# Attention stages at planned places of the expert chunks, batch 1's one unit later, query transposes ahead of the value bounce

## The chip, the cores and the metric

The kernel runs on one core of a Trainium2 chip. The metric is the device time of one execution in microseconds (us), lower is better; the median of three runs is given. The five engines are named as in the profile: PE (TensorE; PEld is its weight load), DVE (VectorE), ACT (ScalarE), POOL (GpSimd), SP (SyncE, which here only issues DMAs). A queue of an engine is worked off strictly in the order in which the program was written, except that a weight load may run ahead.

## The reference, cut to what matters

Sinkhorn-sorted block attention over 4 batches, 8 heads, 768 tokens, head size 64, in 8 blocks of 96 tokens, then 4 experts over 3072 tokens of width 512 with hidden width 1024.

```python
# P: [B,H,8,8], five rounds of softmax over rows and normalisation over columns
k_sorted = einsum('bhij,bhjcd->bhicd', P, k_blocks)   # v_sorted likewise
attn = softmax(q_b @ k_sorted_b.T / 8)                # inside a block of 96
x    = (attn @ v_sorted_b) -> [B*S, H*D]
p    = domain_probs / domain_probs.sum(-1)
out  = sum_e p[:, e] * (relu(x @ w1[e]) @ w2[e])
```

## The kernel before, in words

Batch 0's attention is done first (two halves), in a form of its own. From then on the experts' matmuls fill PE, and the attention of the next batch is put between them in pieces. Everything is scheduled by hand: an engine's queue has the order in which the Python code emits instructions.

**Batch 0's experts** are units `(b, e, hf)` run by `expert`: four groups `ps_h` (8 matmuls, 128x384 each, L548, evicted by ACT as relu) and three groups `ps_o` (8 matmuls of 512 columns, L562, evicted by DVE at L569/L573). A unit has 7 slots, one behind each group. Batch 1's attention is put into the slots of six units, (0,0,1) to (0,3,1).

**Batches 1 to 3** run as three chunks each of 256 tokens, `chunk(b, c)`: eight groups `ps_h` (16 matmuls, L636, two for each expert, evicted by DVE at L642 into `Hb` with relu and the token weights `pb`), then seven products of a Strassen-like scheme (`ps_p`, 16 matmuls each, L663) in the order p1, p4, p2, p5, p6, p7, p3. `h_sums(e, 1..4)` are DVE additions (L617 to L623) of blocks of `Hb` into `Sb`; the products p5, p6, p7 and p3 read sums 1, 2, 3 and 4. `weight_sums(e)` are the additions on the weights' side, on POOL (L596 to L599), one expert after the other. A chunk has 15 slots: one behind each of the 8 groups and of the 7 products. PSUM has two buffers `psM` for `ps_h`, `ps_o` and the products, and two `psA` for the attention.

**The attention stages** of one pair of heads `pr` (four pairs): `st_q` transposes q by a DMA from SP's queue (`qT<-natq`, L324). `st_v` mixes the blocks of v on PE (L298), evicts into `vo` (one buffer; DVE for batch 1, ACT otherwise), and after every second pair writes `vo` to `vs_dram` and reads it back as `vs`, both from SP's queue (L311, L316): the value bounce. `st_k` mixes k (L334), `st_s` makes scores and exponentials (L351, L358 on ACT), `st_a` multiplies by `vs` (L383) and normalizes on DVE (L367, L368), `st_x` transposes the result into `xT` by a DMA from SP. `load_natural` and `load_queries` fetch the next batch's v, k and q by DMAs from POOL's queue, as `load_w1` and `load_w2` do with the experts' weights (L114, L117).

`run` spreads a list of stages evenly over the slots of its units; `attention_order(b)` is that list. `spread_weights` normalizes the token weights of batches 1 to 3 (DVE L512 to L515), transposes them on PE (L530), writes them to `p_dram` (L533) and loads the first `pb` (L606). The same four operations of `normalized` are run on batch 0's smaller table `p_sb` during the start.

Of the kernel before, what the change touches and what calls it, by code (L numbers as in the profile page):

```python
# [17 lines left out]
def kernel(  # L18
# [13 lines left out]
    B, H, S, D = q.shape  # L32
# [4 lines left out]
    E = moe_w1.shape[0]  # L37
# [5 lines left out]
    R = BLK // CP  # L43
    NKC = Dm // P
    NFC = FF // P
    NPB = H // 2
# [39 lines left out]
    def load_natural(b, nm, qd, p0=0, pn=P):  # L86
        src = {"q": q, "k": k, "v": v}[nm]
        if b == 0 and nm == "q":
            natural[(b, nm, qd)] = q0[:, ds(4 * qd, 4)]
        elif (b, nm, qd) not in natural:  # L90
            natural[(b, nm, qd)] = nat.tile([P, 4, R, D], F16, name=f"nat_{nm}_{b}_{qd}", tag=f"nat_{nm}")
        t = natural[(b, nm, qd)]
        nc.gpsimd.dma_start(  # L93
            t[ds(p0, pn)].rearrange("p h r d -> p h (r d)"),
            src[b, ds(4 * qd, 4)].rearrange("h (p r) d -> p h (r d)", r=R)[ds(p0, pn)],
        )

    def load_queries(b):

        t = nat.tile([P, NPB, R, 2, D], F16, name=f"natq_{b}", tag="natq", bufs=1)  # L100
        natural[(b, "q")] = t
        for h in range(H):
            nc.gpsimd.dma_start(t[:, h // 2, :, h % 2, :], q[b, h].rearrange("(t p) d -> p t d", p=P))  # L103
# [369 lines left out]
    def h_x(qd, hf, copy):  # L473
# [8 lines left out]
            ps.rearrange("p n (r c) -> p r n c", c=CP),  # L482
        )

    def attention_order(b):
        o = [(st_v, 0), (st_v, 1), (st_q, 0), (st_k, 0), (st_v, 2), (st_v, 3)]
        for pr in range(NPB):
            o.append((st_s, pr))
            if pr + 1 < NPB:
                o += [(st_q, pr + 1), (st_k, pr + 1)]  # L490
            o.append((st_a, pr))
            o.append((st_x, pr))

        for pr in range(NPB - 1):
            o.remove((st_x, pr))
            o.insert(o.index((st_s, pr + 1)) + 1, (st_x, pr))

        def stage(f, pr):
            f(b, pr)
            nm = {st_k: "k", st_v: "v"}.get(f)  # L500
            if nm and pr % 2 and b + 1 < B:
                load_natural(b + 1, nm, pr // 2)
            if f == st_s and pr == NPB - 1 and b + 1 < B:
                load_queries(b + 1)

        return [lambda f=f, pr=pr: stage(f, pr) for f, pr in o]


    def normalized(p, n, name):
# [79 lines left out]
    def weight_sums(e):  # L589
        t = Tt[e]  # L590
        w = w2sb[e]
        b11, b12 = w[:, 0:KH, 0:DH], w[:, 0:KH, DH:Dm]
        b21, b22 = w[:, KH:NFC, 0:DH], w[:, KH:NFC, DH:Dm]
        t2, t3, n4 = t[:, 0], t[:, 1], t[:, 2]
        tt = nc.gpsimd.tensor_tensor
        tt(t3, b22, b12, ALU.subtract)  # L596
        tt(b12, b12, b11, ALU.subtract)
        tt(t2, b22, b12, ALU.subtract)
        tt(n4, b21, t2, ALU.subtract)  # L599
        Ts.append({  # L600
            "b11": b11, "b21": b21, "b22": b22, "t1": b12, "t2": t2, "t3": t3, "n4": n4,
        })
# [9 lines left out]
    def h_sums(e, which):  # L612
        blk = lambda kh, tok: Hb[:, e, ds(kh * KH, KH), ds(tok * P, P)]
        sm = [Sb[:, n, e].rearrange("p (f x) -> p f x", f=KH) for n in range(4)]
        tt = nc.vector.tensor_tensor
        if which == 1:
            tt(sm[0], blk(0, 1), blk(1, 1), ALU.add)  # L617
        elif which == 2:
            tt(sm[1], sm[0], blk(0, 0), ALU.subtract)
        elif which == 3:  # L620
            tt(sm[2], blk(0, 0), blk(0, 1), ALU.subtract)
        else:
            tt(sm[3], blk(1, 0), sm[1], ALU.subtract)  # L623
# [3 lines left out]
    def chunk(b, c, slot):  # L627

        xT = xTs[b].rearrange("p k i x -> p k (i x)")
        pb = pbs.pop((b, c))  # L630
        for e in range(E):
            for g in range(2):
                ps = psm([P, 4, 2 * P], F32, f"ps_h_{b}_{c}_{e}_{g}")
                for f in range(4):
                    for kc in range(NKC):
                        nc.tensor.matmul(  # L636
                            ps[:, f, :],
                            w1sb[e][:, kc, ds((4 * g + f) * P, P)],
                            xT[:, kc, ds(2 * c * P, 2 * P)],
                            start=(kc == 0), stop=(kc == NKC - 1),  # L640
                        )
                nc.vector.scalar_tensor_tensor(  # L642
                    out=Hb[:, e, ds(4 * g, 4), :], in0=ps[:], scalar=0.0,
                    op0=ALU.max, in1=pb[:, ds(e, 1), :].broadcast_to([P, 4, 2 * P]), op1=ALU.mult,
                )
                if e:
                    h_sums(e - 1, 1 + 2 * g)
                    h_sums(e - 1, 2 + 2 * g)
                slot()
        for w in range(1, 5):  # L650
            h_sums(E - 1, w)
        if (b, c) != (B - 1, R // 2 - 1):
            nxt = (b, c + 1) if c + 1 < R // 2 else (b + 1, 0)
            pbs[nxt] = load_p(*nxt)

        blk = lambda kh, tok: (lambda e, f: Hb[:, e, kh * KH + f, ds(tok * P, P)])
        sm = lambda n: (lambda e, f: Sb[:, n, e, ds(f * P, P)])

        def product(n, lhs, rhs):
            ps = psm([P, DH], F32, f"ps_{n}_{b}_{c}")  # L660
            for e in range(E):
                for f in range(KH):
                    nc.tensor.matmul(  # L663
                        ps[:], lhs(e, f), Ts[e][rhs][:, f, :],
                        start=(e == 0 and f == 0), stop=(e == E - 1 and f == KH - 1),
                    )
            slot()
            return ps[:]

        oa = moeo.tile([P, Dm], F32, name=f"oa_{b}_{c}", tag="oacc")  # L670
        ob = moeo.tile([P, Dm], F32, name=f"ob_{b}_{c}", tag="oacc")
        p1, p5, u2, u3 = [moe.tile([P, DH], F32, name=f"{n}_{b}_{c}", tag=n, bufs=1) for n in ("p1", "p5", "u2", "u3")]
        tt = nc.vector.tensor_tensor
        o = out[ds(b * S, S), :].rearrange("(t p) d -> p t d", p=P)
        oa1, oa2, ob1, ob2 = oa[:, 0:DH], oa[:, DH:Dm], ob[:, 0:DH], ob[:, DH:Dm]
        nc.scalar.copy(p1[:], product("p1", blk(0, 0), "b11"))  # L676
        nc.scalar.copy(ob1, product("p4", blk(1, 1), "n4"))
        tt(oa1, product("p2", blk(1, 0), "b21"), p1[:], ALU.add)
        nc.scalar.copy(p5[:], product("p5", sm(0), "t1"))
        tt(u2[:], product("p6", sm(1), "t2"), p1[:], ALU.add)  # L680
        nc.gpsimd.tensor_tensor(oa2, u2[:], p5[:], ALU.add)  # L681
        tt(u3[:], product("p7", sm(2), "t3"), u2[:], ALU.add)
        nc.gpsimd.tensor_tensor(ob2, u3[:], p5[:], ALU.add)
        tt(ob1, ob1, u3[:], ALU.add)
        nc.sync.dma_start(o[:, 2 * c + 1, :], ob[:])
        tt(oa2, product("p3", sm(3), "b22"), oa2, ALU.add)
        nc.sync.dma_start(o[:, 2 * c, :], oa[:])

    def run(units, slots, fill, spare=4):

        fill, total, done = list(fill), len(fill), [0, 0]

        def slot():
            done[0] += 1
            while fill and done[1] * (slots - spare) < done[0] * total:
                fill.pop(0)()
                done[1] += 1

        for u in units:
            u(slot)  # L700
        for f in fill:
            f()

    def halves(units):
        return [lambda slot, u=u: expert(*u, slot) for u in units]
# [44 lines left out]
    def builds(b):  # L750
        for n in range(2 * b, 2 * b + 2):
            build_PI(nc.gpsimd, n, "v")
            build_PI(nc.gpsimd, n, "k")

    def plain(*fs):
        return [lambda slot: [f() for f in fs]]

    first = attention_order(1)
    run(
        halves([(0, 0, 1), (0, 1, 1)]) + plain(lambda: weight_sums(0), lambda: weight_sums(1))  # L760
        + halves([(0, 2, 0), (0, 2, 1), (0, 3, 0)]) + plain(lambda: weight_sums(2)) + halves([(0, 3, 1)]),
        6 * SLOTS, first[:10] + [spread_weights] + first[10:],
    )
    builds(2)
    weight_sums(3)
    for b in range(1, B):
        fill = attention_order(b + 1) if b + 1 < B else []
        if b > 1 and fill:
            builds(b + 1)
        run(  # L770
            [lambda slot, b=b, c=c: chunk(b, c, slot) for c in range(R // 2)],
            (R // 2) * (2 * E + 7), fill,
        )
# [1 line left out]
_INS = ['q', 'k', 'v', 'sort_net', 'moe_domain_probs', 'moe_w1', 'moe_w2']  # L775
_OUTS = [((3072, 512), 'float32')]
# [25 lines left out]
```

## Time and profile before

| | us |
|---|---|
| median of 3 runs (lowest, highest) | 404.39 (404.01, 405.47) |
| the profiled execution: its time | 406.25 |
| its span in the trace | 404.5 |
| PE busy in the span | 377.1 (93%) |
| DVE, POOL, ACT busy | 231.9, 105.2, 81.6 |
| first expert group of batch 0 | 29.5 |
| unit (0,0,1), the first with batch 1's attention beside it | 61.9 |
| chunk (1,0) begins | 146.3 |
| chunk (2,0) begins | 233.8 |
| chunk (3,0) begins, no attention beside it | 320.9 |

All stage times are starts in the chain of work that ended last, in us from the span's start. The span leaves out what the execution spends around it (1.75 us in the profiled one). PE is the engine that sets the time, so the table is read by stages: where PE stands still, and where its clock is granted at half.

### The profile page before, as it was taken

To read this page: it belongs to the slowest core of one execution; us is meant where nothing else is said; L and a number is where in the kernel's file an instruction comes from. 1 tells how busy PE (TensorE), PEld (TensorE's weight loads), DVE (VectorE), ACT (ScalarE), POOL (GpSimd) and SP (SyncE) were. 2 spreads that over 40 slices of the span, in tenths; PEclk is the share of its full clock that TensorE was granted. 3 is DMA by queue.
4 is the path that set the end of the run, shared out by engine and by line. 5 is a ranking of instruction groups with operands and counts; after the bars stand their busy time and mean duration, and the time that the engine had idled before them with its cause. 6 is when DMAs were issued, how large, how long until landed. Compare 5 with 4: busy or idle time off the path is not lost.

```text
span 404.5 us, 8510 instructions
## 1 busy us (share of the span) xinstructions
PE 377.1 (93%) x3725; PEld 294.9 (73%) x3725; DVE 231.9 (57%) x413; ACT 81.6 (20%) x124; POOL 105.2 (26%) x125
## 2 busy tenths in 40 slices
PE   5679989767999999999999999999999999999996
PEld 5655555333455568888888888888888888888885
DVE  5452544307144349459459569289379385593772
ACT  2344233221244221302201112311120001000000
POOL 8452540007906992020052040100100100101001
PEclk9958999959899999999999999999999999999999
DMA  9999999972427936761269223431122201101101
GB/s 121 194 209 206 111 175 202 217 157 40 96 41 62 173 79 139 165 123 37 73 119 93 71 94 93 122 92 53 45 64 58 71 2 53 53 0 55 53 2 52
DMA packets 70822, 39.07 MB, mean 97 GB/s; under 512 B 42489, under 2 KB 65089, under 8 KB 70785
## 3 DMA queue, kind: packets, MB, share of 16 engines
q0 software_dynamic: 34624, 17.83, 34.0%
q1 hardware_dynamic: 36161, 20.70, 21.2%
q8 instruction: 29, 0.48, 0.5%
q14 instruction: 8, 0.07, 0.1%
HBM read 42.86 MB, written 8.76 MB: 128 GB/s over the span
## 4 chain that ended last, share of the span: by engine, by line
PE 82%; DMA 7%; DVE 7%; ACT 1%; issue 1%; POOL 1%; SPq 0%; DVEq 0%; ACTq 0%; POOLq 0%
PE ps_h L636 29%; PE ps_p L663 28%; PE ps_o L562 9%; PE ps_h L548 9%; DMA vs_dram<-vo 3%; DMA T<-in_q_dram 3%; DVE xsl L368 2%; DVE Hb L642 2%; DMA qT<-natq 2%; PE ps_s L351 1%; PE ps_k L334 1%; PE ps_a L383 1%; PE ps_v L298 1%; PE ps_x L477 1%; ACT ET L451 1%
## 5 line engine op out<-in xcount | busy, mean ns | idle before, releaser
L636 PE MATMUL ps_h<-xT,w 128*128 128x256 f16 x1152 | 131.3, 273 | 1.2 <-DVE Hb L642 1.2
L636 PEld LDWEIGHTS <-w 128*128 128x128 f16 x1152 | 111.9, 98 | 16.5 <-issue 2.2
L642 DVE SCALAR_TENSOR_TENSOR Hb<-ps_h,pb 128x1024 f16<-128x1024 f32 x72 | 87.8, 1220 | 21.5 <-PE ps_h L636 20.3
L663 PEld LDWEIGHTS <-Sb 128*128 128x128 f16 x576 | 55.9, 98 | 6.9
L681 POOL TENSOR_TENSOR oa<-u,p 128x256 f32<-128x256 f32 x9 | 6.5, 724 | 195.8 <-issue 189.2
L548 PE MATMUL ps_h<-xT,w 128*128 128x384 f16 x256 | 49.6, 345 | 0.2 <-ACT xT L480 0.2
L663 PEld LDWEIGHTS <-Hb 128*128 128x128 f16 x432 | 41.8, 98 | 5.9 <-issue 0.6
L562 PE MATMUL ps_o<-w,Hb 128*128 128x512 f16 x192 | 45.0, 388 | 0.0
L554 ACT ACTIVATE Hb<-ps_h 128x768 f16<-128x768 f32 x32 | 26.0, 811 | 66.0 <-PE ps_h L548 66.0
L548 PEld LDWEIGHTS <-w 128*128 128x128 f16 x256 | 25.0, 102 | 17.7 <-issue 3.5
L573 DVE SCALAR_TENSOR_TENSOR oacc<-ps_o,p_sb,oacc 128x512 f32<-128x512 f32 x18 | 13.5, 751 | 40.5 <-PE ps_o L562 40.5
L663 PE MATMUL ps_p<-w,Sb 128*128 128x256 f16 x288 | 34.4, 273 | 0.0
L562 PEld LDWEIGHTS <-Hb 128*128 128x128 f16 x192 | 18.5, 100 | 21.8 <-issue 2.2
L663 PE MATMUL ps_p<-w,Hb 128*128 128x256 f16 x288 | 34.4, 273 | 0.0
L663 PE MATMUL ps_p<-T,Sb 128*128 128x256 f16 x288 | 32.9, 273 | 0.0
L358 ACT ACTIVATE ET<-ps_s 96x768 f16<-96x768 f32 x24 | 18.0, 802 | 42.6 <-PE ps_s L351 42.6
L368 DVE TENSOR_TENSOR xsl<-ps_a,rz 96x512 f16<-96x512 f32 x32 | 22.0, 687 | 1.1
L680 DVE TENSOR_TENSOR u<-ps_p,p 128x256 f32<-128x256 f32 x9 | 3.8, 425 | 29.3 <-PE ps_p L663 29.3
L103 POOL DMA_DIRECT2D natq<-in_q_dram x24 | 19.7, 857 | 0.4 <-issue 0.4
L676 ACT COPY p<-ps_p 128x256 f32<-128x256 f32 x9 | 3.4, 374 | 78.0 <-PE ps_p L663 63.3
L93 POOL DMA_DIRECT2D nat_k<-in_k_dram x8 | 6.4, 795 | 44.9 <-PE ps_k L334 34.7
L663 PE MATMUL ps_p<-T,Hb 128*128 128x256 f16 x144 | 17.2, 272 | 0.1
(98 smaller groups left out, 329.1 us busy)
## 6 DMA issues: line engine op xcount, KB each, us to landing
w<-in_moe_w_dram POOLq DMA_DIRECT2D x8, 1024.0 KB, 17.8
pb<-p_dram SPq DMA_DIRECT2D x9, 512.0 KB, 4.1
nat_k<-in_k_dram POOLq DMA_DIRECT2D x8, 384.0 KB, 5.6
nat_v<-in_v_dram POOLq DMA_DIRECT2D x8, 384.0 KB, 7.3
vs_dram<-vo SPq DMA_DIRECT2D x6, 396.0 KB, 3.7
vs<-vs_dram SPq DMA_DIRECT2D x6, 396.0 KB, 3.7
natq<-in_q_dram POOLq DMA_DIRECT2D x24, 96.0 KB, 5.1
out_dram<-ob SPq DMA_DIRECT2D x9, 256.0 KB, 2.0
```

The source lines that it names most:

```text
L93: nc.gpsimd.dma_start(t[ds(p0, pn)].rearrange("p h r d -> p h (r d)"), src[b, ds(4 * qd, 4)].rearrange("h (p r) d -> p h (r d)", r=R)[ds(p ...
L103: nc.gpsimd.dma_start(t[:, h // 2, :, h % 2, :], q[b, h].rearrange("(t p) d -> p t d", p=P))
L358: nc.scalar.activation(ETs[2 * (pr % 2) + hh][:, 0:S].rearrange("c (a x) -> c a x", a=2), pss[hh][0:BLK, :, 0:HS], AF.Exp, bias=0.0, scale ...
L368: nc.vector.tensor_tensor(xsl[:, :, hh, :].rearrange("c (a i) d -> c a i d", a=2), av[:, :, :, 0:D], rz[:].broadcast_to([BLK, 2, HB, D]), ...
L548: nc.tensor.matmul(ps[:, a, 0:HS], w1sb[e][:, kc, ds((2 * f2 + a) * P, P)], xT0[hf][:, :, kc, :], start=(kc == 0), stop=(kc == NKC - 1),)
L554: nc.scalar.activation(hT[:, ds(2 * f2, 2), :], ps[:, :, 0:HS], AF.Relu, bias=0.0, scale=1.0,)
L562: nc.tensor.matmul(ps[:], hT[:, fc, ds(t * P, P)], w2sb[e][:, fc, :], start=(fc == 0), stop=(fc == NFC - 1),)
L573: nc.vector.scalar_tensor_tensor(out=oaccs[(b, col)][:], in0=ps[:], scalar=pcol, op0=ALU.mult, in1=oaccs[(b, col)][:], op1=ALU.add,)
L636: nc.tensor.matmul(ps[:, f, :], w1sb[e][:, kc, ds((4 * g + f) * P, P)], xT[:, kc, ds(2 * c * P, 2 * P)], start=(kc == 0), stop=(kc == NKC ...
L642: nc.vector.scalar_tensor_tensor(out=Hb[:, e, ds(4 * g, 4), :], in0=ps[:], scalar=0.0, op0=ALU.max, in1=pb[:, ds(e, 1), :].broadcast_to([P ...
L663: nc.tensor.matmul(ps[:], lhs(e, f), Ts[e][rhs][:, f, :], start=(e == 0 and f == 0), stop=(e == E - 1 and f == KH - 1),)
L681: nc.gpsimd.tensor_tensor(oa2, u2[:], p5[:], ALU.add)
```

## The change

Nothing is computed in another way; instructions of attention and of the sums move. Four edits:

1. `spread_weights` runs in the first slot of unit (0,0,1), and nothing else is put beside that unit. Batch 1's attention begins one unit later, in five units instead of six.
2. `attention_order`: `st_q` of pair 0 comes first, ahead of the first two `st_v`; `st_x` follows its `st_a` at once.
3. Batches 2 and 3's attention is put at places (chunk, slot, stage, pair) from a table instead of evenly; `builds(3)` (POOL's mixing matrices) runs behind chunk (1,1).
4. `h_sums`: sum 1 goes behind an expert's first group, sums 2 and 3 behind the second, and sum 4 of all four experts behind product p5.

```diff
     def attention_order(b):
-        o = [(st_v, 0), (st_v, 1), (st_q, 0), (st_k, 0), (st_v, 2), (st_v, 3)]
+        o = [(st_q, 0), (st_v, 0), (st_v, 1), (st_k, 0), (st_v, 2), (st_v, 3)]
         for pr in range(NPB):
             o.append((st_s, pr))
             if pr + 1 < NPB:
                 o += [(st_q, pr + 1), (st_k, pr + 1)]
-            o.append((st_a, pr))
-            o.append((st_x, pr))
-        for pr in range(NPB - 1):
-            o.remove((st_x, pr))
-            o.insert(o.index((st_s, pr + 1)) + 1, (st_x, pr))
+            o += [(st_a, pr), (st_x, pr)]
...
+    PLAN = [
+        (0, 0, st_q, 0), (0, 1, st_v, 0), (0, 2, st_v, 1), (0, 3, st_k, 0), (0, 3, st_q, 1),
...
+        (1, 10, st_x, 1), (1, 12, st_a, 2), (1, 14, st_x, 2),
+        (2, 2, st_s, 3), (2, 8, st_a, 3), (2, 10, st_x, 3),
+    ]
...
                 if e:
-                    h_sums(e - 1, 1 + 2 * g)
-                    h_sums(e - 1, 2 + 2 * g)
+                    for w in ((1,), (2, 3))[g]:
+                        h_sums(e - 1, w)
                 slot()
-        for w in range(1, 5):
+        for w in range(1, 4):
             h_sums(E - 1, w)
...
         nc.scalar.copy(p5[:], product("p5", sm(0), "t1"))
+        for e in range(E):
+            h_sums(e, 4)
         tt(u2[:], product("p6", sm(1), "t2"), p1[:], ALU.add)
...
-    first = attention_order(1)
+    run(halves([(0, 0, 1)]), SLOTS, [spread_weights])
     run(
-        halves([(0, 0, 1), (0, 1, 1)]) + plain(lambda: weight_sums(0), lambda: weight_sums(1))
+        halves([(0, 1, 1)]) + plain(lambda: weight_sums(0), lambda: weight_sums(1))
         + halves([(0, 2, 0), (0, 2, 1), (0, 3, 0)]) + plain(lambda: weight_sums(2)) + halves([(0, 3, 1)]),
-        6 * SLOTS, first[:10] + [spread_weights] + first[10:],
+        5 * SLOTS, attention_order(1),
     )
...
     for b in range(1, B):
-        fill = attention_order(b + 1) if b + 1 < B else []
-        if b > 1 and fill:
-            builds(b + 1)
-        run(
-            [lambda slot, b=b, c=c: chunk(b, c, slot) for c in range(R // 2)],
-            (R // 2) * (2 * E + 7), fill,
-        )
+        for c in range(R // 2):
+            at = [0]
+
+            def slot(b=b, c=c, at=at):
+                for cc, n, f, pr in PLAN:
+                    if b + 1 < B and (cc, n) == (c, at[0]):
+                        stage(b + 1, f, pr)
+                at[0] += 1
+
+            chunk(b, c, slot)
+            if c == 1 and b + 2 < B:
+                builds(b + 2)
```

SP's queue after the start-up loads, before. A name ends in batch and pair (or half) and then a running number: `qT_1_0` is batch 1, pair 0.

```order
L311 DMA vs_dram_309<-vo_0_145 128x6x264
L316 DMA vs_1_0_1074<-vs_dram_309 96x2112
L324 DMA_TRANSPOSE qT_1_0_1098<-natq_1_599 128x6x128
L311 DMA vs_dram_309<-vo_0_145 128x6x264
L316 DMA vs_1_1_1166<-vs_dram_309 96x2112
L324 DMA_TRANSPOSE qT_1_1_1220<-natq_1_599 128x6x128
L533 DMA p_dram_311<-pT_312 18x4x128
L606 DMA pb_1_0_1330<-p_dram_311 128x4x256
```

The same place of SP's queue now:

```order
L538 DMA p_dram_311<-pT_312 18x4x128
L611 DMA pb_1_0_1064<-p_dram_311 128x4x256
L324 DMA_TRANSPOSE qT_1_0_1139<-natq_1_599 128x6x128
L311 DMA vs_dram_309<-vo_0_145 128x6x264
L316 DMA vs_1_0_1170<-vs_dram_309 96x2112
L311 DMA vs_dram_309<-vo_0_145 128x6x264
L316 DMA vs_1_1_1237<-vs_dram_309 96x2112
L324 DMA_TRANSPOSE qT_1_1_1299<-natq_1_599 128x6x128
```

The first query transpose stands ahead of both bounces instead of behind the first, and behind the token weights' write and load; the second stands behind both bounces in either version.

DVE's queue around the normalisation of the token weights, before (it follows the normalisation of attention pair 0 in unit (0,2,0)):

```order
L573 SCALAR_TENSOR_TENSOR oacc_0_5_1145<-ps_o_0_1_5_1258,p_sb_147,oacc_0_5_1145 128x512
L367 RECIPROCAL rz_51_1278<-ps_a_1_0_0_1269 96x8
L368 TENSOR_TENSOR xsl_1_0_1268<-ps_a_1_0_0_1269,rz_51_1278 96x8x64
L367 RECIPROCAL rz_52_1290<-ps_a_1_0_1_1281 96x8
L368 TENSOR_TENSOR xsl_1_0_1268<-ps_a_1_0_1_1281,rz_52_1290 96x8x64
L512 TENSOR_REDUCE den_1_1321<-T_2_84 128x18
L513 TENSOR_SCALAR den_1_1321<-den_1_1321 128x18
L514 RECIPROCAL den_1_1321<-den_1_1321 128x18
L515 TENSOR_TENSOR T_2_84<-T_2_84,den_1_1321 128x72
L531 COPY pT_312<-ps_p_1326 72x128
```

DVE's queue from the end of unit (0,1,0) on, now:

```order
L578 SCALAR_TENSOR_TENSOR oacc_0_2_845<-ps_o_0_1_2_1035,p_sb_147,oacc_0_2_845 128x512
L517 TENSOR_REDUCE den_1_1055<-T_2_84 128x18
L518 TENSOR_SCALAR den_1_1055<-den_1_1055 128x18
L519 RECIPROCAL den_1_1055<-den_1_1055 128x18
L520 TENSOR_TENSOR T_2_84<-T_2_84,den_1_1055 128x72
L536 COPY pT_312<-ps_p_1060 72x128
```

The normalisation moved ahead of all of batch 1's attention, directly behind the last eviction of unit (0,1,0).

DVE's queue at the second pair of value evictions, at the end of unit (0,1,1), now (before, the two `vo` rows stood together, with a `ps_o` eviction of unit (0,0,1) ahead of them):

```order
L578 SCALAR_TENSOR_TENSOR oacc_0_3_1105<-ps_o_0_1_3_1198,p_sb_147,oacc_0_3_1105 128x512
L578 SCALAR_TENSOR_TENSOR oacc_0_4_1116<-ps_o_0_1_4_1208,p_sb_147,oacc_0_4_1116 128x512
L305 CAST vo_0_145<-ps_v_1_2_1218 128x6x2x64
L578 SCALAR_TENSOR_TENSOR oacc_0_5_1127<-ps_o_0_1_5_1222,p_sb_147,oacc_0_5_1127 128x512
L305 CAST vo_0_145<-ps_v_1_3_1232 128x6x2x64
```

An expert eviction now stands between the two; the first `vo` row overwrites the single buffer `vo`, so it waits until the first bounce has been written.

DVE's queue in the products of chunk (1,1), before: nothing between the evictions of p2 and p6.

```order
L678 TENSOR_TENSOR oa_1_1_2407<-ps_p2_1_1_2474,p1_1_1_2409 128x256
L680 TENSOR_TENSOR u2_1_1_2411<-ps_p6_1_1_2530,p1_1_1_2409 128x256
L682 TENSOR_TENSOR u3_1_1_2412<-ps_p7_1_1_2550,u2_1_1_2411 128x256
L684 TENSOR_TENSOR ob_1_1_2408<-ob_1_1_2408,u3_1_1_2412 128x256
L686 TENSOR_TENSOR oa_1_1_2407<-ps_p3_1_1_2571,oa_1_1_2407 128x256
```

And now, the same products:

```order
L683 TENSOR_TENSOR oa_1_1_2421<-ps_p2_1_1_2488,p1_1_1_2423 128x256
L628 TENSOR_TENSOR Sb_124<-Hb_123,Sb_124 128x512 x4
L367 RECIPROCAL rz_86_2576<-ps_a_2_2_0_2567 96x8
L368 TENSOR_TENSOR xsl_2_2_2566<-ps_a_2_2_0_2567,rz_86_2576 96x8x64
L367 RECIPROCAL rz_87_2588<-ps_a_2_2_1_2579 96x8
L368 TENSOR_TENSOR xsl_2_2_2566<-ps_a_2_2_1_2579,rz_87_2588 96x8x64
L687 TENSOR_TENSOR u2_1_1_2425<-ps_p6_1_1_2549,p1_1_1_2423 128x256
L689 TENSOR_TENSOR u3_1_1_2426<-ps_p7_1_1_2593,u2_1_1_2425 128x256
```

The four sums 4 (in every chunk) and the normalisation of attention pair 2 (in chunks (1,1) and (2,1)) stand ahead of p6's eviction.

More of the change, by code (lines that the diff above doesn't have):

```diff
@@ L483, in h_x, with stage @@
         )
+    def stage(b, f, pr):
+        f(b, pr)
+        nm = {st_k: "k", st_v: "v"}.get(f)
+        if nm and pr % 2 and b + 1 < B:
+            load_natural(b + 1, nm, pr // 2)
+        if f == st_s and pr == NPB - 1 and b + 1 < B:
+            load_queries(b + 1)
     def attention_order(b):
-        o = [(st_v, 0), (st_v, 1), (st_q, 0), (st_k, 0), (st_v, 2), (st_v, 3)]
+        o = [(st_q, 0), (st_v, 0), (st_v, 1), (st_k, 0), (st_v, 2), (st_v, 3)]
         for pr in range(NPB):
@@ L490, in attention_order @@
                 o += [(st_q, pr + 1), (st_k, pr + 1)]
-            o.append((st_a, pr))
-            o.append((st_x, pr))
-        for pr in range(NPB - 1):
-            o.remove((st_x, pr))
-            o.insert(o.index((st_s, pr + 1)) + 1, (st_x, pr))
[L498 to L506, printed above, removed]
+            o += [(st_a, pr), (st_x, pr)]
+        return [lambda f=f, pr=pr: stage(b, f, pr) for f, pr in o]
+    PLAN = [
+        (0, 0, st_q, 0), (0, 1, st_v, 0), (0, 2, st_v, 1), (0, 3, st_k, 0), (0, 3, st_q, 1),
+        (0, 4, st_v, 2), (0, 5, st_v, 3), (0, 6, st_s, 0), (0, 9, st_a, 0), (0, 10, st_k, 1),
+        (0, 11, st_x, 0), (0, 12, st_s, 1), (0, 12, st_q, 2),
+        (1, 1, st_k, 2), (1, 5, st_k, 3), (1, 5, st_q, 3), (1, 8, st_a, 1), (1, 10, st_s, 2),
+        (1, 10, st_x, 1), (1, 12, st_a, 2), (1, 14, st_x, 2),
+        (2, 2, st_s, 3), (2, 8, st_a, 3), (2, 10, st_x, 3),
+    ]
     def normalized(p, n, name):
```

## The prediction

> **What bounds the kernel now.** PE is busy for 93% of the span, so the first view is who waited for whom, for the rows where PE waits; the second the chain of work that ended last, for where these waits lie; the third the granted clock.
>
> The waits (us in total, times, longest):
>
> ```profile
> PE ps_s L351 <- DMA qT<-natq: 6.4, 1, 6.4
> PE ps_p L530 <- DVE T L515: 2.9, 1, 2.9
> DVE u L680 <- PE ps_p L663: 29.3, 9, 3.6
> ```
>
> Behind the start-up PE stands still for long only twice: 6.4 us for batch 1's first transposed q, 2.9 us for the normalized token weights. The chain shows why (start, us, what):
>
> ```profile
> 58.42 3.46 PE ps_o L562 x16
> 61.88 1.30 PE ps_h L548 x8
> 63.18 0.33 PE ps_v L298 x2
> ...
> 65.17 0.97 DVE vo L305
> 66.22 10.66 DMA vs_dram<-vo
> 76.90 0.33 SPq L316
> 77.33 7.06 DMA qT<-natq
> 84.44 0.82 PE ps_s L351 x9
> 85.26 2.67 PE ps_h L548 x8
> 87.94 4.80 PE ps_o L562 x16
> ...
> 101.01 0.40 PE ps_p L530
> 101.41 2.56 PE ps_h L548 x8
> ...
> 146.32 1.75 PE ps_h L636 x16
> ```
>
> The transpose of q waited on SP behind the value bounce's read, which waited 10.66 us for the write. Behind both waits matmuls take about double: a `ps_h` group 2.67 or 2.56 us instead of 1.30. The stages (us, busy times, PE's granted clock, DMA share) confirm the clock:
>
> ```profile
> 62.00:85.00 23.00, 16.58 (x116) 9.16 (x113) 7.53 (x9) 5.68 (x7) 1.50 (x2) 0.90 1.21 218
> 101.00:104.00 3.00, 2.99 (x13) 1.30 (x15) 0.29 (x1) 0.00 (x0) 3.00 (x2) 0.50 0.07 18
> 320.90:347.40 26.50, 26.48 (x242) 23.41 (x240) 17.74 (x29) 1.12 (x3) 1.45 (x2) 1.00 0.13 41
> ```
>
> The DMA engines are full up to 85 us (share 1.21). A chunk with no attention takes 26.5 us at full clock. What the filled chunks of batches 1 and 2 lose is small (term 5: 1.2 us of waits); the six units before them lose over 13.
>
> **Term 1, the query transpose (edits 1 and 2).** It costs 6.4 idle, and at half clock 2.67 - 1.30 = 1.4 and 4.80 against 2 x 1.73 = 3.46, 1.3 more: 9.1 us. Now it stands on SP behind the token weights' write and load. When does PE want it? PE runs `ps_h` to 63.2, waits 0.5 for the weights (term 2) and transposes them, 64.1; three `ps_h` and three `ps_o` groups (1.30 and 1.73) end unit (0,0,1) at 73.2; unit (0,1,1) with four `ps_v` (0.33), one `ps_k` (0.46) and 0.1 lost at each change ends at 85.9; one `ps_h` more, and `ps_s` is due at 87.3. When does it come? Two rows of DMA issues (size, us to landing; the second is the last of the experts' weights) and that one's issue on POOL:
>
> ```profile
> T<-in_moe_domain_probs_dram SPq DMA_DIRECT2D x1, 36.0 KB, 15.4
> w<-in_moe_w_dram POOLq DMA_DIRECT2D x1, 1024.0 KB, 24.2
> 54.23 0.98 POOL L117 DMA_DIRECT2D w<-in_moe_w_dram  x1
> ```
>
> The weights' write is issued at about 64.6. For its landing nothing is the lower bound; the 36 KB load of the same table at the full start, 15.4, is the upper. I take the bounce's 10.7, the nearest in queue and stage though of 396 KB: 75.3, `pb` issued by 75.7, then q with its 7.1: 82.8. Even 15.4 gives 87.5. The last expert weights land at 54.2 + 24.2 = 78.4, early enough for unit (0,2,0) at 85.9. So the wait goes: -9.1.
>
> **Term 2, the normalisation (edit 1).** DVE and POOL rows around it, and the same operations on batch 0's table:
>
> ```profile
> 27.86 0.17 DVE L513 TENSOR_SCALAR den<-den 128x6 f32<-128x6 f32 x1
> 28.30 0.18 DVE L515 TENSOR_TENSOR p_sb<-p_sb,den 128x24 f32<-128x24 f32 x1
> 61.92 0.75 DVE L573 SCALAR_TENSOR_TENSOR oacc<-ps_o,p_sb,oacc 128x512 f32<-128x512 f32 x1 [0.97 <-PE ps_o L562]
> 96.46 2.12 POOL L597 TENSOR_TENSOR w<-w 128x1024 f16<-128x1024 f16 x1
> 97.65 0.97 DVE L513 TENSOR_SCALAR den<-den 128x18 f32<-128x18 f32 x1
> 98.66 2.12 POOL L598 TENSOR_TENSOR T<-w 128x1024 f16<-128x1024 f16 x1
> 98.95 1.92 DVE L515 TENSOR_TENSOR T<-T,den 128x72 f32<-128x72 f32 x1
> ```
>
> L513 and L515 took 0.97 and 1.92 us for 18 and 72 columns, against 0.17 and 0.18 for 6 and 24, and each ended just behind a POOL addition (98.62 behind 98.58, 100.87 behind 100.78): DVE stood behind `weight_sums`. At 62.7, behind L573, POOL has no additions (its last work is the weight load's issue at 54.23; `weight_sums` needs unit (0,1,1) to end). The four operations then take about 0.9 us (three of them took 0.62 on the small table, 27.86 to 28.48), and PE, there at 63.2, waits about 0.5 instead of 2.9; an idle that short leaves the clock alone. Before it cost 2.9 + (2.56 - 1.30) = 4.2, now 0.5: -3.7.
>
> The Trainium skill (TensorE: Matmul & The Clock Gate, What's actually happening) lets the clock fall only after an idle window of about 3.4 us. The trace differs: 2.9 us of idle, then 0.50 granted. By the page the term would be -2.4 instead of -3.7; the row decides.
>
> **Term 3, the bounce one unit later.** DVE's third `vo` waits for the first write, and behind it stand `ps_o`'s eviction and the fourth `vo`, for which `ps_s` waits since it needs both attention buffers. In turn 0.97 + 0.75 + 0.97 (L305, L573), about 2.8 us with gaps: a write landing later than 84.5 delays `ps_s`. The DMA rows (last number: us to landing) give the median of the six writes, and the one issued at 78.85 by itself:
>
> ```profile
> vs_dram<-vo SPq DMA_DIRECT2D x6, 396.0 KB, 3.7
> vs_dram<-vo SPq DMA_DIRECT2D x1, 396.0 KB, 7.0
> ```
>
> It is issued at about 79.2 (`ps_v` of pair 1 ends at 78, eviction 1.0). A landing in 10.7, as with full engines at 66.22, gives 5.4 us of wait and 2.7 of slow clock; 7.0, when the last weights came in beside it, 1.7; 3.7 none. The weights are in by then but a value load runs beside the write, so I take the middle of the two nearer rows: +0.8. The second q transpose, still behind both bounces, comes at about 97 by these rows and is due at 99.6: nothing.
>
> **Term 4, the end of batch 1's attention.** ACT's exponentials by group, `xT`'s landing, and from the chain one normalisation:
>
> ```profile
> L358 ACT ACTIVATE ET<-ps_s 96x768 f16<-96x768 f32 x24 | 18.0, 802 | 42.6 <-PE ps_s L351 42.6
> xT<-xsl SPq DMA_TRANSPOSE x12, 3.0
> ...
> 212.49 0.21 DVE rz L367
> 213.55 0.69 DVE xsl L368
> ```
>
> `ps_a` of pair 3 follows its scores after one `ps_h` (1.3 us), while ACT needs two exponentials of 0.8: +0.2. After `ps_a` come three `ps_h` and three `ps_o`, 9.1 us; normalizing takes 1.75 (212.49 to 214.24) and `xT` 3.0 to land, so chunk (1,0) doesn't wait for it: nothing.
>
> **Term 5, the chunks (edits 3 and 4).** What PE loses to DVE goes, 1.2 us in three waits. From the groups the `ps_h` matmuls (last: idle before them), from the chain pair 3's `ps_k` of batch 1, from the timeline POOL's last `weight_sums` and the DVE sum beside it, and the group of sums 4:
>
> ```profile
> L636 PE MATMUL ps_h<-xT,w 128*128 128x256 f16 x1152 | 131.3, 273 | 1.2 <-DVE Hb L642 1.2
> 124.40 0.46 PE ps_k L334 x12
> ...
> 151.87 2.13 POOL L599 TENSOR_TENSOR T<-w,T 128x1024 f16<-128x1024 f16 x1
> 153.46 0.82 DVE L617 TENSOR_TENSOR Sb<-Hb 128x512 f16<-128x512 f16 x1
> L623 DVE TENSOR_TENSOR Sb<-Hb,Sb 128x512 f16<-128x512 f16 x36 | 15.1, 418 | 0.0
> ```
>
> An expert gives DVE two evictions and three sums now, so it keeps closer to PE. Two costs come in. In chunks (1,1) and (2,1) p6's eviction stands behind a normalisation (1.75): its buffer comes free 2.6 us after p6, and p3 wants it after `ps_a` and p7, 2.2: +0.4 twice. And L617 took 0.82 instead of 0.42 while POOL's last addition ran to 154.0. POOL ended 154.0 - 124.9 = 29.1 us after pair 3's `ps_k`; chunk (1,0) now begins 18.7 us behind that (21.5 before), so the additions reach 10.4 us into the chunk instead of 7.7 and two places of sums stand behind them: I find +0.3 from the buffers, up to 2.1 (one addition) if nothing hides it. The Trainium skill (SBUF — State Buffer, Who interferes with whom) has a rule for it, which speaks against the change: a DVE instruction with two SBUF inputs and a POOL one that reads SBUF block each other for a whole instruction; L617's row agrees. Sum: -1.2 + 0.8 + 0.3 = -0.1. The four sums 4 (4 x 0.42 = 1.7) hide beside p5 and p6: DVE waited 29.3 / 9 = 3.3 us per chunk there.
>
> **The sum.** -9.1 - 3.7 + 0.8 + 0.2 - 0.1 = -11.9 us. The profiled execution goes from 406.25 (span 404.5 and 1.75 around it) to 394.3; the median lies 1.86 under it, so 404.39 becomes 392.5.
>
> **The rivals.**
> - The bounce takes q's place as the wait: the write lands in 10.7 us as before. For it: the first one did. Against: the weights were still landing then. 392.5 - 0.8 + 8.1 = 399.8, less for anything between.
> - DVE's normalisation is slow by its size. For it: 72 columns against 24. Against: ends that coincide with POOL's. Term 2 is lost: 396.2.
> - The change doesn't free q: SP's line holds it. If the weights' write takes 15.4 and q moves only behind all of `pb` (10.7), it comes at 91 + 3.8 = 95, 7.6 too late with 2.7 of slow clock: 402.8, no change. Against: the write is a ninth or less of a bounce's bytes.
> - The other side: the four sums 4 aren't hidden. They stand ahead of p6's eviction, and if DVE reaches them when p6 is already done, each of nine chunks pays 1.7, 15 us: 407.8, slower. It decides once DVE is over 1.8 us behind at p5. Against: its wait of 3.3 us at that place.
>
> **How the numbers follow.** The forecast has 0.68, with its own range 390 to 395; the bounce 0.14, the slow normalisation 0.07, q held 0.04, the sums 0.04; 0.03 is left for what I don't see. The low end, 389.8, has no bounce wait, no new chunk waits (-0.8 - 1.1) and a normalisation that is hidden (-0.5) and takes -0.3 for term 4; the high end, 399.8, is the bounce at 10.7. About 0.5%, 2 us, is what a measurement here tells from no change. Under 402.4 lie the forecast, the bounce and the normalisation, and half of the unseen: 0.91; within 0.5% q held: 0.04; above 406.4 the sums: 0.05.
>
> **What would show it.** Right: no wait of PE for `qT`, one of under 1 us for L520, L520 under 0.4 us, chunk (1,0) starting near 134.5, clock 1.00 from 62 us on. Term 3: a wait of DVE `vo` for `vs_dram`, and of PE's `ps_s` behind it. Term 5: PE waits for u of p6 in chunks (1,1) and (2,1). Wrong if PE stands over 3 us anywhere behind 62 us, since the slow clock then doubles the price.

## The result and the profile after

The changed kernel takes 392.34 us (median of four runs, 392.05 to 392.97), the kernel before on the same chip 404.28 (four runs). The ratio is 0.970, with a 95% interval of 0.968 to 0.972: faster by 3.0%, 11.9 us. The profiled execution took 392.05 us with a span of 390.3. That of before took 406.25, 1.9 above its median, so the spans differ by 14.2 us and the medians by 11.9; this gap turns out to matter.

The page of the kernel after:

```profile
span 390.3 us, 8513 instructions
...
L641 PE MATMUL ps_h<-xT,w 128*128 128x256 f16 x1152 | 130.3, 273 | 0.0
```

The `ps_h` matmuls of the chunks (L636 before) have lost their 1.2 us of idle time, and 1.0 us of busy time too. The second has a meaning, below.

The waits of PE behind 60 us and two of DVE's (us in total, times, longest):

```profile
PE ps_s L351 <- DVE vo L305: 1.3, 1, 1.3
PE ps_p L535 <- DVE T L520: 0.6, 1, 0.6
PE ps_p L668 <- DVE u L687: 0.4, 2, 0.2
...
DVE u L687 <- PE ps_p L668: 12.8, 7, 2.2
```

The wait of 6.4 for `qT` is gone, the one for the weights is 0.6 instead of 2.9. Two small ones are new. DVE still waits for the products, now up to 2.2 us at p6 instead of 3.6: the four sums 4 stand in what was its spare time.

The chain of work that ended last (start, us, what):

```profile
63.55 0.27 PE ps_p L535
63.82 3.90 PE ps_h L553 x24
...
77.49 0.97 DVE vo L305
...
78.51 6.91 DMA vs_dram<-vo
...
86.42 0.74 DVE oacc L578
87.16 0.88 DVE vo L305
...
88.08 0.50 PE ps_s L351 x15
...
134.37 3.49 PE ps_h L641 x32
```

Three `ps_h` groups behind the transpose of the weights take 3.90, three times 1.30: full clock. The bounce's write takes 6.91, and the third `vo`, `ps_o`'s eviction and the fourth `vo` follow it one by one to `ps_s`. Chunk (1,0) begins at 134.37 instead of 146.32.

Two stretches of the profile (us, busy times of PE, PEld, DVE, ACT and POOL, granted clock, DMA share, GB/s; the first is the same stretch of time as before, the second one chunk of batch 3):

```profile
62.00:85.00 23.00, 22.45 (x133) 11.77 (x131) 8.22 (x14) 6.49 (x8) 0.76 (x1) 1.00 1.13 190
307.76:333.96 26.20, 26.20 (x243) 23.48 (x241) 17.74 (x29) 1.12 (x3) 1.45 (x2) 1.00 0.12 41
```

The clock stays at 1.00. And a chunk of batch 3, where no attention runs and no wait was listed before, takes 26.2 us; before, such chunks start 26.57 us apart (320.85 and 347.42 in the chain). That gain was not in the prediction.

**Where the time went, by two stages.** Of the traces used below, three have batch 1's attention as before and four as after. From the first `ps_h` of unit (0,0,1) to chunk (1,0) the first three take 84.60 (before: 61.72 to 146.32), 81.85 (before again) and 83.17 (the sums alone); the others 72.83 (after), 72.78 (after again), 72.46 (old sums) and 72.26 (old spread). The means are 83.2 and 72.6: 10.6 us. That size goes with the execution of before that is taken. The rest doesn't: from chunk (1,0) to the end of the span both traces of before take 258.2 us and both of after 255.9. The chain gives it to a hundredth: to the start of the last eviction it is 254.36 and 254.35 against 252.10 in both, so there the gain, 2.25 us, repeats to a hundredth.

### The profile page after: what moved, and what is told of

Read it like the earlier page. It is cut to its first block, busy times and chain, and to the rows that moved or that the text cites. A ratio compares the mean times of both kernels' runs of the same rounds, so it can differ in the third digit from the quotient of the medians.

```text
span 390.3 us, 8513 instructions
## 1 busy us (share of the span) xinstructions
PE 370.9 (95%) x3725; PEld 293.0 (75%) x3725; DVE 230.7 (59%) x413; ACT 81.7 (21%) x124; POOL 105.2 (27%) x125
## 4 chain that ended last, share of the span: by engine, by line
PE 88%; DMA 4%; DVE 4%; ACT 1%; POOL 1%; issue 1%; DVEq 0%; SPq 0%; ACTq 0%; POOLq 0%
PE ps_h L641 33%; PE ps_p L668 28%; PE ps_h L553 10%; PE ps_o L567 9%; DMA T<-in_q_dram 3%; DMA vs_dram<-vo 2%; PE ps_a L383 1%; DVE xsl L368 1%; PE ps_s L351 1%; PE ps_k L334 1%; PE ps_v L298 1%; PE ps_x L477 1%; ACT ET L451 1%; PE ps_s L444 1%; DVE kT L417 0%
## 5 line engine op out<-in xcount | busy, mean ns | idle before, releaser
L553 PE MATMUL ps_h<-xT,w 128*128 128x384 f16 x256 | 46.7, 332 | 0.2 <-ACT xT L480 0.2
L567 PE MATMUL ps_o<-w,Hb 128*128 128x512 f16 x192 | 43.8, 379 | 0.0
L93 POOL DMA_DIRECT2D nat_v<-in_v_dram x8 | 6.1, 761 | 37.9 <-PE ps_v L298 31.5
```

The source lines that it names most:

```text
L93: nc.gpsimd.dma_start(t[ds(p0, pn)].rearrange("p h r d -> p h (r d)"), src[b, ds(4 * qd, 4)].rearrange("h (p r) d -> p h (r d)", r=R)[ds(p ...
L553: nc.tensor.matmul(ps[:, a, 0:HS], w1sb[e][:, kc, ds((2 * f2 + a) * P, P)], xT0[hf][:, :, kc, :], start=(kc == 0), stop=(kc == NKC - 1),)
L567: nc.tensor.matmul(ps[:], hT[:, fc, ds(t * P, P)], w2sb[e][:, fc, :], start=(fc == 0), stop=(fc == NFC - 1),)
```

## The experiments

**Before again.** The kernel before, unchanged, profiled once more: how much of the stage's 84.6 us is of that one execution?

> The kernel before, profiled a second time. Its first profiled execution took 406.25 us, 2.0 more than the median of its runs, while the changed kernel's profiled one is like its median; so the two traces differ by 14.2 us of span and the medians by 11.9. Theory A: the first trace caught a long wait for the transposed q (a DMA time); this one shows the same pure chunks of batch 3 (26.5 us each, 79.8 together) and a q wait of 4 to 5 us instead of 6.4. Rival B: the 2 us lie in PE's own pace or the granted clock somewhere else, and the q wait is 6.4 again.

404.44 us, span 402.7 (before on this chip: 405.87, median of 15; each ratio below is against runs of before on the same chip). The chain:

```profile
85.53 0.82 PE ps_s L351 x16
86.35 2.54 PE ps_h L548 x8
88.90 3.45 PE ps_o L562 x16
...
98.56 1.93 DVE T L515
...
100.62 0.28 PE ps_p L530
100.90 1.30 PE ps_h L548 x8
```

PE waited 6.6 us for q and 2.9 for the weights, as in the first trace. But behind the first wait only one `ps_h` group was slow (2.54, the two `ps_o` at full speed with 3.45), and behind the second none: 1.30, where the first trace had 2.56. The waits repeat, and the half clock behind them doesn't. It cost 4.0 us in the first trace and 1.2 here, as rival B had it; what decides it stands in the last section.

**The sums alone.** The kernel before with edit 4 only:

```diff
-                    h_sums(e - 1, 1 + 2 * g)
-                    h_sums(e - 1, 2 + 2 * g)
+                    for w in ((1,), (2, 3))[g]:
+                        h_sums(e - 1, w)
...
-        for w in range(1, 5):
+        for w in range(1, 4):
...
+        for e in range(E):
+            h_sums(e, 4)
```

> Before plus edit 4 alone (sum 1 behind the first group, sums 2 and 3 behind the second, sums 4 behind p5). Theory A: in every chunk PE loses about 0.37 us to DVE in steps too short to be shown as idle (in batch 3, chunks of 26.57 us before and 26.20 after); edit 4 takes it away in nine chunks, with the three listed waits of 1.2 us: -2.5 to -4 us, and batch 3's chunks at 26.2. Rival B, the forecast's reading: only the listed waits exist, batch 3 has nothing to give: -0.5 to -1.2 us, chunks of batch 3 at 26.6.

401.95 us, 0.992 of before (0.988 to 0.995), 3.4 us less by the ratio. From chunk (1,0) to the end the trace has 255.4 instead of 258.2: 2.8 us, of which the listed waits were 1.2. Batch 3 in the chain, before and here:

```profile
320.85 14.12 PE ps_h L636 x128
334.96 1.80 PE ps_p L663 x16
336.78 10.64 PE ps_p L663 x96
```

```profile
317.63 13.97 PE ps_h L636 x128
331.60 12.23 PE ps_p L663 x112
```

Eight `ps_h` groups take 13.97 instead of 14.12, and seven products 12.23 instead of 12.44: 0.36 us for a chunk. The timeline of before shows where (PE and DVE between a chunk's `ps_h` and its products), and behind it that of after:

```profile
361.43 1.91 PE L663 MATMUL ps_p<-w,Hb 128*128 128x256 f16 x16
...
362.09 1.22 DVE L642 SCALAR_TENSOR_TENSOR Hb<-ps_h,pb 128x1024 f16<-128x1024 f32 x1
...
363.36 1.91 PE L663 MATMUL ps_p<-T,Hb 128*128 128x256 f16 x16
```

```profile
347.77 1.91 PE L668 MATMUL ps_p<-w,Hb 128*128 128x256 f16 x16
347.98 1.23 DVE L647 SCALAR_TENSOR_TENSOR Hb<-ps_h,pb 128x1024 f16<-128x1024 f32 x1
...
349.52 1.91 PE L668 MATMUL ps_p<-T,Hb 128*128 128x256 f16 x16
```

Both products show 1.91 us. But from the start of p1 to the start of p4 it is 1.93 us before and 1.75 after: p4 reads the last `Hb`, which came at 363.31. A group's end is modelled 0.16 us beyond the point where the next can start, so a wait shorter than that leaves no idle time; it hides in the busy time. Batch 3's three chunks had 1.1 us of this. So edit 4 is worth 2.8 us, not the 1.2 that the waits list.

**The weights alone.** The kernel before with `spread_weights` first, the attention still from unit (0,0,1) on:

```diff
-        6 * SLOTS, first[:10] + [spread_weights] + first[10:],
+        6 * SLOTS, [spread_weights] + first,
```

> Before plus the token weights' normalisation in the first slot of unit (0,0,1), nothing else. Theory A: with POOL idle there the normalisation's last operation takes 0.2 instead of 1.9 us, PE waits about 0.6 instead of 2.9 us for it and the slow clock behind it goes: -3.7 us at that place; the q wait stays behind the bounce, 5 to 8 us, since the weights' write and load now stand ahead of both on SP: -2 to -4 us in all. Rival B: the operation is slow by its size: no gain, PE waits 3 us at the new place. Rival C: the two additional DMAs push the bounce back and the q wait eats the gain: -1 to +3.

403.16 us, 0.993 (0.991 to 0.995). PE's waits:

```profile
PE ps_s L351 <- DMA qT<-natq: 7.7, 1, 7.7
...
PE ps_p L530 <- DVE T L515: 0.6, 1, 0.6
```

The four operations are short by their place and not by their size: 0.6 of wait with the same 72 columns. About 1.2 us of the gain goes into the wait for q (7.7, against 6.4 and 6.6 in the two traces of before), since the bounce now stands on SP behind the weights' write, is issued at 70.67 instead of 66.22 and takes 11.63.

**The query first, alone.** The kernel before with edit 2's first line:

```diff
-        o = [(st_v, 0), (st_v, 1), (st_q, 0), (st_k, 0), (st_v, 2), (st_v, 3)]
+        o = [(st_q, 0), (st_v, 0), (st_v, 1), (st_k, 0), (st_v, 2), (st_v, 3)]
```

> Before plus edit 2's first half alone: the first query transpose first in the list, no unit's delay, normalisation where it was. Theory A: q waits only for SP's queue; the wait of 4 to 6.4 us and the half clock behind it (2.7) go: -6.5 to -9 us; the wait for the normalized weights (2.9, with its slow clock) stays. Rival B: the DMA engines are full up to 80 us, so q comes late all the same, or the values for the first attention product come late instead: -3 us or less, PE waiting 4 us or more for qT or vs.

399.74 us, 0.985 (0.980 to 0.990), 6 us less, a little under the least that was expected. The wait for `qT` is gone, and the one for `vo` stands in its place:

```profile
PE ps_s L351 <- DVE vo L305: 3.0, 2, 2.4
PE ps_p L530 <- DVE T L515: 2.9, 1, 2.9
```

The bounce's write, issued at 69.44, took 10.44 us there.

**The unit's delay undone.** The changed kernel with batch 1's attention from unit (0,0,1) on, behind the weights:

```diff
-    run(halves([(0, 0, 1)]), SLOTS, [spread_weights])
-        halves([(0, 1, 1)]) + plain(lambda: weight_sums(0), lambda: weight_sums(1))
+        halves([(0, 0, 1), (0, 1, 1)]) + plain(lambda: weight_sums(0), lambda: weight_sums(1))
...
-        5 * SLOTS, attention_order(1),
+        6 * SLOTS, [spread_weights] + attention_order(1),
```

> The changed kernel without the unit's delay: batch 1's attention spread over six units from (0,0,1) on, the weights' normalisation and the first query transpose still in front. Theory A: the delay matters because the bounce then meets full DMA engines: its first write is issued near 74 behind the transpose and lands in 7 to 11 us, the third vo eviction on VectorE waits for it, and PE waits 3 to 6 us for the first scores with half clock behind it: +3 to +8 us against the changed kernel. Rival B: the delay buys nothing once q stands first: within 1 us.

398.37 us, 0.982 (0.979 to 0.986): 6 us of the gain lost against the changed kernel's 0.967 on the same chip (below), 5 against the 0.970 of the result. From unit (0,0,1) to chunk (1,0) its trace takes 79.04 us instead of 72.8. The chain:

```profile
73.70 10.67 DMA vs_dram<-vo
...
85.37 0.96 DVE vo L305
86.36 0.80 PE ps_s L351 x15
87.16 4.93 PE ps_o L567 x16
```

A write issued at 73.70, with the experts' weights still landing (the last load, issued at 54.08, takes 24.0), takes 10.67; the one at 78.51 takes 6.91. PE waits 5.5 us for the fourth `vo`, and the two `ps_o` behind it take 4.93 instead of 3.46. This is the rival of the bounce, made true by a place 5 us earlier.

**POOL beside the normalisation.** The changed kernel with three more additions on POOL, started when DVE reaches the normalisation (a copy of a word of `oacc`'s makes them wait):

```diff
+    def busy_weights():
+        nc.gpsimd.tensor_copy(mark[:], oaccs[(0, 2)][:, 0:1])
+        for _ in range(3):
+            w0 = w2sb[0]
+            nc.gpsimd.tensor_tensor(Tt[0][:, 1], w0[:, KH:NFC, DH:Dm], w0[:, 0:KH, DH:Dm], ALU.subtract)
+        spread_weights()
...
-    run(halves([(0, 0, 1)]), SLOTS, [spread_weights])
+    run(halves([(0, 0, 1)]), SLOTS, [busy_weights])
```

> The changed kernel with three more additions on POOL (each like the first of weight_sums, 2.1 us, reading weights from SBUF and writing a tile that is written again later) that start when the last eviction of unit (0,1,0) ends, so beside the normalisation of the token weights. Theory A: VectorE's operations with SBUF inputs stand behind POOL's additions: the tensor_scalar and the last multiplication end at the ends of POOL's additions, PE waits 3 to 4 us instead of 0.55, with half clock behind it: +3.5 to +6 us against the changed kernel. Rival B: the normalisation is fast because of its place, not because POOL is idle: no change (within 0.5 us).

395.2 us, 0.974 (0.971 to 0.978): 2.9 us more than the changed kernel's 0.967 on the same chip (below), and less than expected. The trace says the same: 75.74 us from unit (0,0,1) to chunk (1,0) instead of 72.8. The timeline, in order of engines, and the chain behind it:

```profile
63.73 6.50 POOL L771 TENSOR_TENSOR T<-w 128x1024 f16<-128x1024 f16 x3
...
63.69 0.17 DVE L518 TENSOR_SCALAR den<-den 128x18 f32<-128x18 f32 x1
...
64.20 1.73 DVE L520 TENSOR_TENSOR T<-T,den 128x72 f32<-128x72 f32 x1
...
66.08 0.27 PE L535 MATMUL ps_p<-T 128*72 128x128 f32 x1 [2.04 <-DVE T L520]
```

```profile
66.35 5.58 PE ps_h L553 x24
```

L520 takes 1.73 us, nearly the 1.92 of before, until the first of three additions ends at about 65.9; alone it took 0.24. L518 had started before the additions, so one operation was held and not two: that is what the expectation had too large. PE waits 2.0 us, and the three `ps_h` behind it take 5.58 instead of 3.90, the slow clock behind a shorter wait than the 2.9 that three traces passed without it.

**The old spread of batches 2 and 3.** The changed kernel with edit 3 undone:

```diff
-        for c in range(R // 2):
...
-            chunk(b, c, slot)
+        fill = attention_order(b + 1) if b + 1 < B else []
+        if b > 1 and fill:
+            builds(b + 1)
+        run(
+            [lambda slot, b=b, c=c: chunk(b, c, slot) for c in range(R // 2)],
+            (R // 2) * (2 * E + 7), fill,
+        )
```

> The changed kernel with edit 3 undone: batches 2 and 3's attention spread evenly over the slots again and builds(3) where it was. Theory A: the table brings nothing by itself: the waits of PE for p6's eviction (0.4 twice) go, waits of PE for the evictions of ps_h come back in part, since normalisations stand among them again: within 1 us of the changed kernel. Rival B: the table is what brings the chunks' 1.1 us in batches 1 and 2: +1 us or more.

393.7 us, 0.971 (0.967 to 0.974). Against the changed kernel's 0.970 that is nothing; but on this chip the changed kernel took 391.72 (below), and all six runs here lie above its four. The trace has 257.7 us from chunk (1,0) to the end instead of 255.9, with four waits of PE for `Hb`, 1.5 us in all. So beside the other edits the table is worth about 1.8 us, as rival B had it. Against the old places it earns nothing: before with edit 4 alone takes 255.4 us there, less than the changed kernel. The even spread loses only in company with the new order of stages and the later unit; no run parts those two.

**The old places of the sums.** The changed kernel with edit 4 undone (the diff of the sums alone, turned round), and beside it on the same chip **the changed kernel again**:

> The changed kernel with edit 4 undone (all four sums behind the groups and in front of p1 again). Theory A, from the two traces of before and the run of edit 4 alone: each chunk of batch 3 goes back from 26.20 to 26.57 us, and in batches 1 and 2 VectorE falls behind again: +2 to +4 us against the changed kernel. Rival B: with the attention at planned places the old sums fit too, and only batch 3 loses: +1.1 us.

> The changed kernel itself, on the same chip and in the same rounds as the one with the old sums, as the yardstick for it, and a second trace of it: the same waits of PE (0.4 to 0.6 for the weights, 0.9 to 1.4 for the scores, 0.4 for p3) and no stretch of half clock behind 62 us. If the trace differs by more than 1 us anywhere, single traces can't carry terms of that size.

395.5 us, 0.976 (0.973 to 0.978), and 391.72, 0.967 (0.965 to 0.969). Edit 4 is worth 3.4 us by the ratios; from chunk (1,0) to the end, 258.8 instead of 255.9, it is 2.9. Most of that falls in one place. The chain of the old sums:

```profile
140.59 1.23 DVE Hb L647
141.81 1.59 DVE Sb L622
...
143.42 2.23 DVE Sb L624
145.65 1.15 DVE Hb L647
...
146.84 1.91 PE ps_h L641 x16
```

Two sums of 128x512, 0.41 us each elsewhere, stand beside POOL's last additions and take 1.59 and 2.23; the eviction behind them comes late, and PE waits 1.7 us. Batch by batch, batch 1 takes 88.50 us with the old sums and 86.74 with the new, batch 2 86.67 and 86.66: with the attention at planned places edit 4 brings nothing there, and batch 3 has the other 1.1. With the new places the sums in that stretch (DVE, then POOL, of the kernel after) are:

```profile
141.18 1.66 DVE L622 TENSOR_TENSOR Sb<-Hb 128x512 f16<-128x512 f16 x1
142.76 1.21 DVE L647 SCALAR_TENSOR_TENSOR Hb<-ps_h,pb 128x1024 f16<-128x1024 f32 x1
143.90 1.21 DVE L624 TENSOR_TENSOR Sb<-Sb,Hb 128x512 f16<-128x512 f16 x1
...
142.64 2.19 POOL L604 TENSOR_TENSOR T<-w,T 128x1024 f16<-128x1024 f16 x1
```

An eviction now stands between the two, and no wait of PE is listed there.

**What is left of the waits.** The changed kernel with a second buffer for `vo` (a part of `Sb` that is unused until the chunks), the weights one slot later and one `st_a` one slot earlier:

```diff
-        vo = vos[0]
+        vo = vo2 if b == 1 and pr >= 2 else vos[0]
...
-        (1, 10, st_x, 1), (1, 12, st_a, 2), (1, 14, st_x, 2),
+        (1, 10, st_x, 1), (1, 11, st_a, 2), (1, 14, st_x, 2),
...
-    run(halves([(0, 0, 1)]), SLOTS, [spread_weights])
+    vo2 = Sflat[:, 0:R * 4 * VW].rearrange("p (r h w) -> p r h w", r=R, h=4)
+    nc.gpsimd.memset(vo2[:, :, :, ds(D, 2)], 1.0)
+    run(halves([(0, 0, 1)]), SLOTS, [lambda: None, spread_weights])
```

> The changed kernel with its three remaining waits taken away: the normalisation of attention pair 2 one product earlier (slot 11, behind p5, which ACT evicts), the token weights one slot later (two groups cover the normalisation), and a second vo buffer for batch 1's second pair of values. Theory A: -0.55, -1.3 and -0.8: -2 to -3 us against the changed kernel, none of the three waits in the trace. Rival B: the waits move elsewhere (the bounce's second write, q's second transpose): -1 us or less.

390.15 us, 0.962 (0.959 to 0.964), against 0.970 and 0.967 of the changed kernel's two comparisons, so 2.3 us less than that on the same chip: the best of all versions here. Behind 50 us the trace lists one wait of PE, in batch 0:

```profile
PE ps_x L477 <- ACT ET L451: 1.1, 1, 1.1
```

Unit (0,0,1) to chunk (1,0) takes 70.73 us instead of 72.8, the chunks 255.2 instead of 255.9: mostly the two waits of 1.3 and 0.6, and the two of 0.2 with what hid beside them.

## Why the prediction was right, point by point

392.5 was forecast and 392.34 measured. The mechanisms of terms 1 to 4 held. The sizes of the waits' slow clock and of term 5 were off, in opposite directions, and that the figure is so close is luck.

- **Term 1 (-9.1), the query.** Right in kind: no wait for `qT`, whose transpose was issued at 71.10 and landed some 9.4 us later, where 82.8 was forecast and 87.3 due. Its size was that of one execution: 6.4 of wait repeats (6.6 and 7.1 in the two other traces with the old order), the 2.7 of slow clock was 1.2 and 2.0 in those.
- **Term 2 (-3.7), the normalisation.** L520 took 0.24 us and PE waited 0.55, as forecast, and the POOL block that it rested on was made again by the additions put beside it. But the 1.3 us of slow clock behind the old wait of 2.9 was 0 in all three other traces that have this wait (before again, the sums alone, the query first alone). So in three of four traces the term is 2.9 - 0.5 = 2.4.
- **Here the Trainium skill was weighed and put aside for the row.** Its page "TensorE: Matmul & The Clock Gate" (What's actually happening) lets the clock fall after an idle window of about 3.4 us and calls that window free-running. By it the term was -2.4, and that is what three of four traces show; I should have taken the row as one draw. The traces agree that the window runs free: the clock here changes on a grid of 3.41 us steps (last section). They differ on the length: 2.0 us of idle was followed by half clock in the run with POOL busy, so a wait below that figure of the Trainium skill is no safe place either.
- **Term 3 (+0.8), the bounce.** The write was issued at 78.51 (79.2 forecast) and landed in 6.91, the upper of the two near rows; DVE waited 2.0 us and PE 1.3. Size 0.5 too small, mechanism as told. The experts' weights were not quite in: the last load, issued at 54.02, took 25.8 us, to about 79.8.
- **Term 4 (+0.2).** Pair 3's `ps_a` took 0.66 us instead of 0.48. Chunk (1,0) began at 134.37, forecast 134.5.
- **Term 5 (-0.1), the chunks.** The step that failed: "What PE loses to DVE goes, 1.2 us in three waits." It measured -2.25. Edit 4 was worth 2.8, since waits too short to be listed went too, 1.1 us of them in batch 3 alone. The costs: p3's two waits came, at 0.2 instead of 0.4. The port block of the later unit costs nothing listed beside the new sums, where 0.3 was taken, but without edit 4 it would have been 1.7, near the 2.1 that the prediction gave as its bound. So the edits lean on each other: with the old sums the later unit and the table leave the chunks 0.6 us longer than before (258.8 against 258.2). With the new sums they still cost some: all edits gain 2.25 where edit 4 alone gains 2.8, so the others take back about 0.5, where 1.1 was forecast. The rows of 2.23 and 1.73 agree with the Trainium skill's rule on the shared port (SBUF — State Buffer, Who interferes with whom).
- **The sum.** Terms 1 to 4 gave -11.8 for a stage that lost 11.8 against the trace it was made from (84.60 to 72.83), but 10.6 between the means of the traces, and 9.7 by the medians of the result (11.9 less the 2.25 of the chunks). So terms 1 to 4 were 1.2 to 2.1 too much, and term 5 was 2.15 too little; at the upper figure the two cancel. On another chip they don't: there the medians are 404.83 and 391.72 (the changed kernel again), a gain of 13.1. Taking the sum from an execution 1.9 us above the median and subtracting it from the median carried its slow clock along. What the three old traces lose to the waits and the clock, 13.3, 10.7 and 12.0, leaves 71.3, 71.2 and 71.2 of their stage: the waits and the clock are all that differs between them.
- **The rivals.** The bounce at 10.7 is real 5 us earlier (the delay undone), not here. The slow normalisation is refuted by the weights alone. q wasn't held: the weights' write was done by 70.6, 6.4 us behind its issue instead of the 10.7 that I took. The four sums 4 are hidden: DVE waits for p6 behind them.

## What to carry to other kernels

To see what an engine loses to its feeders, read from start to start of equal groups as well as the listed waits: a modelled end hides every wait shorter than its overhang, and of the 2.8 us that edit 4 gained in the kernel before the list had 1.2. Price a wait that repeats by its length, and the slow clock behind it by more than one execution. When a transfer is moved, look at what else is landing then: the same write took 10.7 us at 73.7, while the experts' weights came in, and 6.9 at 78.5, at their end. No run here moved only the other loads, so that they are the cause is argued and not shown.

## What the hardware showed that I had not expected

- **Half clock behind idle time goes by a grid, not by the length of the wait.** Behind waits of 0.55 and 1.3 us: none. Behind 2.0: +1.7 us. Behind 2.4: +1.1. Behind 2.9: +1.3 once, 0 three times. Behind 5.5 to 7.7: +1.2 to +2.7. The traces show what decides. In each of them the granted clock changes only at points that lie whole steps of 3.41 us apart. Here is the wait of 2.9, cut at these points, in the first trace of before (PE idle from 98.1 to 101.0) and then in the second (97.7 to 100.6); the columns are those of the stretches above:

```profile
97.36:100.77 3.41, 0.75 (x5) 0.23 (x3) 3.31 (x5) 1.17 (x2) 3.33 (x2) 1.00 0.17 27
100.77:104.18 3.41, 3.17 (x17) 1.50 (x19) 0.39 (x2) 0.11 (x1) 3.33 (x3) 0.50 0.06 16
```

```profile
95.46:98.87 3.41, 2.26 (x14) 1.16 (x12) 3.24 (x8) 1.62 (x2) 3.25 (x3) 1.00 0.69 109
98.87:102.28 3.41, 1.66 (x17) 0.97 (x19) 1.90 (x2) 0.00 (x0) 3.33 (x2) 1.00 0.00 0
```

In the first, 2.66 us of the wait fall into one step, and the next step runs at 0.50. In the second the wait is split into 1.15 and 1.75, and the clock stays at 1.00, in the next step too. Behind 30 us the twelve traces have 1229 steps at full clock. The eight in which PE was idle for 2.05 us or more were each followed by a step at half clock, and none of the others, with 1.96 or less. The grid lies elsewhere in each execution, so the same wait of 2.9 us pays in one and not in the next.
- **A small DVE operation can be held for a whole POOL addition**: 0.24 became 1.73 us for 72 columns, 0.41 became 2.23 for an addition of 512.
